# Fused local-global attention and gated long convolution on one core: the filter's spectrum and the inverse tables move into the attention of batch 0

## The chip, the cores and the metric

The kernel runs on one core of a Trainium2 chip. The metric is the device time of one execution in microseconds. A profile is one execution recorded by the hardware profiler; its span is the time from the first to the last recorded instruction.

## What is computed

Inputs q, k, v are (4, 8, 768, 64): 4 batches, 8 heads, 768 positions, 64 features. Attention is causal and local over 96 positions, plus the first 8 positions for everybody, with a slope per head times the distance as bias:

```python
is_global = pos[None, :] < 8
is_local = (rel >= 0) & (rel < 96)
keep = is_global | is_local
dist = where(is_global & ~is_local, 96, abs(rel))
scores = q @ k.T / 8 - slope[h] * dist
a = softmax(where(keep, scores, -1e9))
x = (a @ v), heads side by side: (4, 768, 512)
```

Its output goes through a gated long convolution ("Hyena"), with one filter for all batches:

```python
x1, x2, x3 = split(x @ w_proj)                 # 512 to 3 * 512
conv = irfft(rfft(x2) * rfft(filter_fft))      # along the 768 positions
out = (x1 * conv * x3) @ w_out                 # float32
```

## The kernel before

**Tiles and stages.** Keys and values of a batch are held in seven tiles of 128 rows: rows 0 to 7 of each tile are the 8 global positions, rows 8 to 127 are 120 positions of their own. For each pair of heads, attention transposes queries and keys on PE (`transpose_q`, `transpose_k`), makes scores in three groups (`weights`, L497), takes the exponential on ACT (L504), multiplies by a mask on DVE (`masked`, L513 and L516, put off by one step), multiplies by the values (`values`, L524 and L529), divides by the sum (L533, L534), and transposes the result into `xT` (`transpose_x`, L541 and L542). After two pairs, `butterfly` (L444, L445) adds and subtracts the two halves of the sequence into `xa` and `xb`; the last butterfly of a batch is what `hyena` reads first (L573).

`hyena` projects `xa` and `xb` with the middle third of `w_proj` (L573, L575), transforms them by matrices (`forward`, L328, six slots: four of 128 frequency rows, two of 64 and 64), multiplies by the filter's spectrum h1, h2 (`product`, `sums`, L588 to L598), transforms back with the inverse tables (L637), multiplies by the gates (`gate`, L559 to L564, with the outer thirds of `w_proj`), and multiplies by `w_out` (L655 to L659).

**The filter stage.** `filter_stage` is ten steps: one that adds and subtracts the filter's halves (L342, L343), six `forward` steps whose result is written into h1 and h2 with scales and signs (L349 to L365), and three that transpose the forward tables into the inverse ones (`inverse_tables`, L287 to L294).

**The order of the work.** Each engine runs its instructions in the order in which the program emits them. `weave` mixes several generators: each gets a start, an end and a number of steps, and the one with the smallest share so far emits the next step. `after(n, fn)` puts a piece of work off: with n = 1 it is emitted at the end of the next woven step. Attention 0 runs alone (L709). Then for each batch b, `hyena` of b and attention of b + 1 are woven (L712 to L723); for b = 0 the filter stage is a third stream with a start at 0.12 and an end at 0.4, and `hyena` emits four gates early. In attention 0 a dummy matmul (`busy`, L280) follows each step.

**PSUM.** `mm` gives out three buffers; in attention 0 the transposes use these too (`tr`), later ones have a buffer of their own.

**Queues.** Nearly all loads go through GpSimd's queue (POOL in the profile), because they convert float32 to float16: values 0, two pairs of heads, the three thirds of `w_proj` (`load_weights`), then `load_batch(1)`: keys 1, queries 1, the filter, values 1; then `w_out`, then batch 2. The 8 global rows of tiles 1 to 6 are copied from tile 0: for batches 1 to 3 by a DMA on SP's queue (L111), for batch 0 by a DVE copy inside attention (L424). The loads of tiles 1 to 6 take 128 rows, of which the first 8 are then overwritten. Keys and queries of batch 0 come in another layout and are not touched by the change.

Of the kernel before, what the change touches and what calls it, by code (L numbers as in the profile page):

```python
# [17 lines left out]
P = 128  # L18
# [26 lines left out]
class Fused:  # L45
# [53 lines left out]
    def load_tiles(self, dst, src, b):  # L99

        g, D = self.nc.gpsimd, self.D
        for t in range(7):
            lo = max(0, self.K0[t] - NG)
            hi = self.K0[t] + KL
            g.dma_start(dst[P - (hi - lo):P, t, :, 0:D],  # L105
                        src[b, :, lo:hi, :].rearrange("h p d -> p h d"))
            if t == 0:
                g.dma_start(dst[0:NG, 0, :, 0:D],
                            src[b, :, 0:NG, :].rearrange("h p d -> p h d"))
        if b > 0:  # L110
            self.nc.sync.dma_start(dst[0:NG, 1:7], dst[0:NG, 0:1].to_broadcast(  # L111
                [NG, 6] + list(dst.shape[2:])))

    def load_batch(self, b):
        g = self.nc.gpsimd
        qt, kt, vt = self.batch_tiles()
        self.load_tiles(kt, self.k, b)
        for t in range(6):
            g.dma_start(qt[:, t], self.q[b, :, P * t:P * t + P, :].rearrange("h p d -> p h d"))  # L119
        if b == 1:  # L120
            self.load_filter()
        self.load_tiles(vt, self.v, b)
        return qt, kt, vt
# [37 lines left out]
    def load_weights(self):  # L161
        g, cp, DM = self.nc.gpsimd, self.cp, self.DM
        self.w = cp.tile([P, 4, 3 * DM], F16)
        self.wr = self.w_proj.rearrange("(t p) n -> p t n", p=P)
        for o in (DM, 0, 2 * DM):
            g.dma_start(self.w[:, :, o:o + DM], self.wr[:, :, o:o + DM])
# [115 lines left out]
    def inverse_tables(self):  # L282
# [3 lines left out]
        for sp in range(3):  # L286
            tp = self.ps.tile([P, 1024], F16, tag="tr", bufs=1)  # L287
# [48 lines left out]
    def filter_spectrum(self):  # L336
# [10 lines left out]
        sc = 2.0 * H_SCALE  # L347

        def evac(s, pt):  # L349
            if s < 4 and s % 2 == 0:  # L350
                nc.scalar.mul(self.h1[:, s], pt, sc)
                nc.vector.tensor_scalar(self.h1[:, s + 1], pt, sc, None, op0=Alu.mult)
                if s == 0:
                    nc.scalar.mul(self.h1[0:1, 0], pt[0:1], H_SCALE)
            elif s < 4:
                nc.scalar.mul(self.h2[:, s - 1], pt, sc)
                nc.vector.tensor_scalar(self.h2[:, s], pt, -sc, None, op0=Alu.mult)
                if s == 1:
                    nc.scalar.mul(self.h1[0:1, 1], pt[0:1], H_SCALE)
# [402 lines left out]
```

## Time and profile before

| | |
|---|---|
| timed runs, us | 221.43, 223.82, 224.78 (median 223.82) |
| profiled execution, us | 222.22 |
| its span, us | 220.4 |
| PE busy | 193.8 us (88%) |
| DVE busy | 148.5 us (67%) |
| ACT busy | 153.3 us (70%) |
| POOL busy | 75.8 us (34%) |
| granted TensorE clock, mean | 0.997 |
| loaded and stored by DMA | 20.90 MB |

A row of the view by groups reads: line, engine, operation, output <- input, shapes and count, then busy us and mean ns of one, then the engine's idle time before them and what ended it. A row of the timeline begins with the start and the length in us; what stands in brackets is the idle time before it and the releaser. Buffer names carry numbers: h_814 is h1, h_815 is h2, f_793 and f_794 are the filter's sum and difference.

### The profile page before, as it was taken

The page shows a single profiled execution, that of the slowest core. Times are in us where ns is not written, and L with a number is a line of the kernel's source. Part 1 is how long each engine was busy: PE and PEld are TensorE (multiplying, and loading weights), DVE is VectorE, ACT ScalarE, POOL GpSimd, SP SyncE. Part 2 cuts the span into 40 slices and gives each one's busy share as a digit, 9 for nine tenths or more (in the row PEclk, how much of TensorE's full clock was granted, in tenths as well). Part 3 has the DMA queues.
Part 4 walks back from the last instruction along what each step waited for, and adds up shares of the span by engine and source line. Part 5 has one row for each costly group of instructions (what it writes and reads, how often), then busy time and mean ns, then how long its engine had stood idle before and what let it go on. Part 6 is the DMA issues. An engine that isn't in the chain of part 4 may idle for free.

```text
span 220.4 us, 4260 instructions
## 1 busy us (share of the span) xinstructions
PE 193.8 (88%) x1661; PEld 104.5 (47%) x1661; DVE 148.5 (67%) x321; ACT 153.3 (70%) x249; POOL 75.8 (34%) x102
## 2 busy tenths in 40 slices
PE   7588986897798968689899999998999999998982
PEld 2243554443455535334455656444555555454630
DVE  6966677564695999822299999334998991078630
ACT  6996685487656767547978685767877847673742
POOL 7999379758795000599540000000000000000000
PEclk9999999999999999999999999999999999999998
DMA  6999999999999800299999000520000006100025
GB/s 195 145 140 184 207 155 155 192 128 166 155 137 122 32 9 3 17 150 231 212 130 39 8 3 1 190 98 0 3 0 3 0 1 241 48 0 0 3 84 204
DMA packets 79573, 20.90 MB, mean 95 GB/s; under 512 B 71328, under 2 KB 76480, under 8 KB 79552
## 3 DMA queue, kind: packets, MB, share of 16 engines
q0 software_dynamic: 74672, 12.46, 91.3%
q1 hardware_dynamic: 4880, 8.16, 11.0%
q8 instruction: 13, 0.21, 0.4%
q14 instruction: 8, 0.07, 0.1%
HBM read 26.48 MB, written 6.29 MB: 149 GB/s over the span
## 4 chain that ended last, share of the span: by engine, by line
PE 31%; DVE 30%; DMA 18%; POOL 8%; ACT 7%; issue 4%; POOLq 0%; DVEq 0%; SPq 0%
PE pt L655 7%; PE pt L559 7%; DMA w<-in_moe_w_proj_dram 5%; DMA vt<-in_v_dram 5%; PE pt L573 5%; DVE g L564 5%; DVE xn L534 4%; DMA fl<-in_moe_filter_fft_dram 4%; DMA vt<-vt 3%; PE pt L637 3%; POOL qt L119 2%; ACT E_104 L504 2%; PE sp L497 2%; DVE E_107 L516 2%; PE pt L328 2%
## 5 line engine op out<-in xcount | busy, mean ns | idle before, releaser
L559 PE MATMUL pt<-xT,w 128*128 128x384 f16 x256 | 46.8, 326 | 0.6 <-DVE g L564 0.4
L559 PEld LDWEIGHTS <-w 128*128 128x128 f16 x256 | 23.4, 98 | 16.7 <-issue 2.5
L105 POOL DMA_DIRECT2D vt<-in_v_dram x28 | 25.2, 913 | 7.6 <-DMA qt<-in_q_dram 4.0
L504 ACT ACTIVATE E_107<-sp 128x864 f16<-128x864 f32 x24 | 21.5, 894 | 7.1 <-PE sp L497 6.6
L655 PE MATMUL pt<-wo,y 128*128 128x512 f16 x96 | 22.2, 379 | 2.6 <-DVE y L648 1.7
L497 PE MATMUL sp<-QT,KT 64*128 64x216 f16 (+2 forms) x224 | 18.2, 254 | 5.9 <-ACT E_104 L504 2.8
L658 ACT ACTIVATE t<-pt 128x512 f32<-128x512 f32 x24 | 14.3, 597 | 13.0 <-PE pt L655 12.9
L504 ACT ACTIVATE E_104<-sp 128x864 f16<-128x864 f32 x24 | 21.5, 897 | 2.4 <-PE sp L497 1.8
L105 POOL DMA_DIRECT2D kt<-in_k_dram x21 | 19.6, 953 | 5.8 <-DMA w<-in_moe_w_proj_dram 4.8
L534 DVE TENSOR_TENSOR xn<-o,rc 128x448 f16<-128x448 f32 x32 | 20.0, 624 | 1.1
L637 PE MATMUL pt<-inv,X 128*128 128x384 f16 x96 | 18.5, 326 | 1.1 <-DVE X L598 1.1
L575 ACT CAST dst<-pt 128x512 f16<-128x512 f32 x24 | 14.2, 593 | 6.8 <-PE pt L573 6.8
L497 PEld LDWEIGHTS <-KT 64*128 64x128 f16 x224 | 7.7, 95 | 23.6 <-issue 19.5
L328 PE MATMUL pt<-dst,fwd 128*128 128x512 f16 x72 | 18.9, 380 | 0.0
L542 ACT COPY xT<-tr 128x768 f16<-128x768 f16 x16 | 12.8, 798 | 7.7 <-PE tr L541 7.6
L601 ACT CAST X<-pt 128x512 f16<-128x512 f32 x24 | 14.1, 588 | 5.5 <-PE pt L328 5.1
L280 PE MATMUL pt<-idle 128*128 128x512 f16 x35 | 16.4, 475 | 1.4 <-DVE warm L682 1.2
L516 DVE TENSOR_TENSOR E_104<-E_104,mask 128x864 f16<-128x864 f16 x16 | 9.7, 604 | 10.4 <-ACT E_104 L504 9.9
L119 POOL DMA_DIRECT2D qt<-in_q_dram x18 | 15.8, 916 | 1.2 <-DMA kt<-in_k_dram 1.1
L655 PEld LDWEIGHTS <-y 128*128 128x128 f16 x96 | 8.9, 98 | 13.3 <-DVE y L648 2.9
L486 DVE COPY KT<-tr 128x896 f16<-128x896 f16 x12 | 7.4, 619 | 10.9 <-PE tr L485 10.9
L541 PE MATMUL tr<-ident,xn 128*128 128x128 f16 x112 | 9.0, 220 | 5.2 <-DVE xn L534 4.8
(231 smaller groups left out, 381.9 us busy)
## 6 DMA issues: line engine op xcount, KB each, us to landing
out_dram<-t SPq DMA_DIRECT2D x24, 256.0 KB, 2.4
vt<-in_v_dram POOLq DMA_DIRECT2D x24, 128.0 KB, 7.4
kt<-in_k_dram POOLq DMA_DIRECT2D x18, 128.0 KB, 7.5
qt<-in_q_dram POOLq DMA_DIRECT2D x18, 128.0 KB, 7.2
w<-in_moe_w_proj_dram POOLq DMA_DIRECT2D x3, 512.0 KB, 10.3
t<-in_q_dram SPq DMA_DIRECT2D x2, 384.0 KB, 4.2
t<-in_k_dram SPq DMA_DIRECT2D x2, 384.0 KB, 5.2
fl<-in_moe_filter_fft_dram POOLq DMA_DIRECT2D x1, 768.0 KB, 9.3
```

The source lines that it names most:

```text
L105: g.dma_start(dst[P - (hi - lo):P, t, :, 0:D], src[b, :, lo:hi, :].rearrange("h p d -> p h d"))
L119: g.dma_start(qt[:, t], self.q[b, :, P * t:P * t + P, :].rearrange("h p d -> p h d"))
L280: self.nc.tensor.matmul(pt, self.idle[:, 0:P], self.idle, start=True, stop=True)
L328: self.nc.tensor.matmul(pt, self.fwd[:, kt, s, :], src[:, kt, :], start=(kt == 0), stop=(kt == 2))
L497: nc.tensor.matmul(sp[:, hh, off:off + w], KT[64 * hh:64 * hh + 64, o:o + P], QT[64 * hh:64 * hh + 64, KL * m:KL * m + w], start=(off == 0 ...
L504: nc.scalar.activation(eo, sp[:, :, 0:432].rearrange("p h (m w) -> p h m w", m=2), Act.Exp, scale=self.scale)
L534: nc.vector.tensor_mul(xn[:, :, hh, :], o[:, :, 0:D], rc.to_broadcast([P, 7, D]))
L559: nc.tensor.matmul(pt[:, 0:h], self.w[:, c, o + P * j:o + P * j + P], xT[:, c, h * s:h * s + h], start=(c == 0), stop=(c == 3))
L575: nc.scalar.copy(dst[:, t, :], pt)
L637: nc.tensor.matmul(pt[:, 0:h], X[:, s, cs], self.inv[:, s, :], start=(s == slots[0]), stop=(s == slots[-1]))
L655: nc.tensor.matmul(pt, y[:, c, P * t:P * t + P], self.wo[:, c, :], start=(c == 0), stop=(c == 3))
L658: nc.scalar.mul(ot, pt, osc)
```

## The change

- The filter stage is woven into attention 0, from the share 0.7 to 1 of it, instead of into Hyena 0; Hyena 0 no longer emits four gates early. The inverse tables' transposes use the three `mm` buffers.
- The filter's load is issued behind the first third of `w_proj`, ahead of keys 1. The two outer thirds (the gates' weights) and `w_out` are issued behind values 1.
- The 8 global rows are loaded first, tiles 0 to 6 take 120 rows each, and the copy to tiles 1 to 6 is a DMA on SP's queue for all batches, batch 0 among them; the DVE copy L424 is gone.
- In the filter stage, each PSUM result is read once by one engine (ACT for h1 of slots 0, 2, 4, 5, DVE for h2); the second copy, or the one with the other sign, is made by DVE from the float16 result in SBUF, partly put off by one step (`second`). The special first row gets its scale from two small per-row tables.

```diff
--- before.py
+++ after.py
@@ -99,17 +99,13 @@
     def load_tiles(self, dst, src, b):
 
         g, D = self.nc.gpsimd, self.D
+        g.dma_start(dst[0:NG, 0, :, 0:D], src[b, :, 0:NG, :].rearrange("h p d -> p h d"))
+        self.nc.sync.dma_start(dst[0:NG, 1:7], dst[0:NG, 0:1].to_broadcast(
+            [NG, 6] + list(dst.shape[2:])))
         for t in range(7):
-            lo = max(0, self.K0[t] - NG)
-            hi = self.K0[t] + KL
-            g.dma_start(dst[P - (hi - lo):P, t, :, 0:D],
-                        src[b, :, lo:hi, :].rearrange("h p d -> p h d"))
-            if t == 0:
-                g.dma_start(dst[0:NG, 0, :, 0:D],
-                            src[b, :, 0:NG, :].rearrange("h p d -> p h d"))
-        if b > 0:
-            self.nc.sync.dma_start(dst[0:NG, 1:7], dst[0:NG, 0:1].to_broadcast(
-                [NG, 6] + list(dst.shape[2:])))
+            lo = self.K0[t]
+            g.dma_start(dst[NG:P, t, :, 0:D],
+                        src[b, :, lo:lo + KL, :].rearrange("h p d -> p h d"))
 
     def load_batch(self, b):
         g = self.nc.gpsimd
@@ -117,9 +113,11 @@
         self.load_tiles(kt, self.k, b)
         for t in range(6):
             g.dma_start(qt[:, t], self.q[b, :, P * t:P * t + P, :].rearrange("h p d -> p h d"))
+        self.load_tiles(vt, self.v, b)
         if b == 1:
-            self.load_filter()
-        self.load_tiles(vt, self.v, b)
+            for part in (0, 2):
+                self.load_w_in(part)
+            self.load_w_out()
         return qt, kt, vt
 
     def load_first(self):
@@ -159,11 +157,12 @@
         return t
 
     def load_weights(self):
-        g, cp, DM = self.nc.gpsimd, self.cp, self.DM
-        self.w = cp.tile([P, 4, 3 * DM], F16)
-        self.wr = self.w_proj.rearrange("(t p) n -> p t n", p=P)
-        for o in (DM, 0, 2 * DM):
-            g.dma_start(self.w[:, :, o:o + DM], self.wr[:, :, o:o + DM])
+        self.w = self.cp.tile([P, 4, 3 * self.DM], F16)
+        self.load_w_in(1)
+
+    def load_w_in(self, part):
+        o, wr = part * self.DM, self.w_proj.rearrange("(t p) n -> p t n", p=P)
+        self.nc.gpsimd.dma_start(self.w[:, :, o:o + self.DM], wr[:, :, o:o + self.DM])
 
     def load_filter(self):
         g, DM = self.nc.gpsimd, self.DM
@@ -284,7 +283,7 @@
         nc = self.nc
         self.inv = self.cp.tile([P, 6, 384], F16)
         for sp in range(3):
-            tp = self.ps.tile([P, 1024], F16, tag="tr", bufs=1)
+            tp = self.tr(True)
             for c in range(2):
                 for a in range(3):
                     nc.tensor.transpose(tp[:, 384 * c + P * a:384 * c + P * a + P],
@@ -345,24 +344,34 @@
         self.h1 = cp.tile([P, 6, DM], F16)
         self.h2 = cp.tile([P, 6, DM], F16)
         sc = 2.0 * H_SCALE
+        s0, s1 = (self.sp.tile([P, 1], F32, bufs=1, name=f"s{i}") for i in range(2))
+        for t, x in ((s0, H_SCALE), (s1, 0.0)):
+            nc.vector.memset(t, sc)
+            nc.vector.memset(t[0:1], x)
+
+        c, a, h = self.h1, self.h2, slice(0, 64)
+
+        def second(s):
+
+            if s < 4:
+                nc.vector.tensor_scalar(a[:, s], a[:, s - 1], -1.0, None, op0=Alu.mult)
+            else:
+                nc.vector.tensor_copy(c[64:P, s], c[h, s])
+                nc.vector.tensor_scalar(a[64:P, s], a[h, s], -1.0, None, op0=Alu.mult)
 
         def evac(s, pt):
             if s < 4 and s % 2 == 0:
-                nc.scalar.mul(self.h1[:, s], pt, sc)
-                nc.vector.tensor_scalar(self.h1[:, s + 1], pt, sc, None, op0=Alu.mult)
-                if s == 0:
-                    nc.scalar.mul(self.h1[0:1, 0], pt[0:1], H_SCALE)
+                nc.scalar.mul(c[:, s], pt, sc if s else s0)
             elif s < 4:
-                nc.scalar.mul(self.h2[:, s - 1], pt, sc)
-                nc.vector.tensor_scalar(self.h2[:, s], pt, -sc, None, op0=Alu.mult)
+                nc.vector.tensor_scalar(a[:, s - 1], pt, sc if s > 1 else s1, None, op0=Alu.mult)
+                nc.vector.tensor_copy(c[:, s], c[:, s - 1])
                 if s == 1:
-                    nc.scalar.mul(self.h1[0:1, 1], pt[0:1], H_SCALE)
-                    nc.vector.memset(self.h2[0:1, 0:2, :], 0.0)
+                    nc.vector.tensor_scalar(c[0:1, 1], pt[0:1], H_SCALE, None, op0=Alu.mult)
             else:
-                nc.scalar.mul(self.h1[0:64, s], pt[0:64], sc)
-                nc.scalar.mul(self.h1[64:P, s], pt[0:64], sc)
-                nc.vector.tensor_scalar(self.h2[0:64, s], pt[64:P], sc, None, op0=Alu.mult)
-                nc.vector.tensor_scalar(self.h2[64:P, s], pt[64:P], -sc, None, op0=Alu.mult)
+                nc.scalar.mul(c[h, s], pt[h], sc)
+                nc.vector.tensor_scalar(a[h, s], pt[64:P], sc, None, op0=Alu.mult)
+            if s % 2 or s == 4:
+                self.after(1, lambda: second(s))
         for s in range(6):
             self.forward(s, f2[0], f2[1], evac)
             yield 1
@@ -420,9 +429,6 @@
         cast(1)
         yield 1
         for i in range(n + 1):
-            if first and i == 1:
-                self.nc.vector.tensor_copy(vt[0:NG, 1:7], vt[0:NG, 0:1].to_broadcast(
-                    [NG, 6, self.H, self.D + 1]))
             for live, fn in ((i < n, lambda: sc(i, 0)),
                              (i + 1 < n, lambda: trk(i + 1)),
                              (i < n, lambda: sc(i, 1)),
@@ -705,15 +711,14 @@
         self.load_tiles(qkv[2], self.v, 0)
         self.load_pairs(2, nc.gpsimd, F16)
         self.load_weights()
+        self.load_filter()
         x = self.new_x()
-        self.weave((self.attention(*qkv, *x, first=(cast, ths)), 34, 0, 1))
+        self.weave((self.attention(*qkv, *x, first=(cast, ths)), 34, 0, 1),
+                   (self.filter_stage(), 10, 0.7, 1))
         loads = [qkv, self.load_batch(1)]
-        self.load_w_out()
         for b in range(self.B):
-            streams = [(self.hyena(b, *x, early=4 if b == 0 else 0), 30, 0, 1)]
+            streams = [(self.hyena(b, *x, early=0), 30, 0, 1)]
             nx = None
-            if b == 0:
-                streams.insert(0, (self.filter_stage(), 10, 0.12, 0.4))
             if b + 2 < self.B:
                 loads.append(self.load_batch(b + 2))
             if b + 1 < self.B:
```

## The prediction

> **What bounds the kernel now.** I read the busy time stage by stage first, because the page's 88% for PE is a mean over unlike stages. Columns: PE, PEld, DVE, ACT, POOL busy us (instructions), granted clock, DMA share, GB/s.
>
> ```profile
> 31.65:41.50 9.85, 7.42 (x105) 4.57 (x106) 6.39 (x15) 5.48 (x8) 9.62 (x12) 1.00 2.18 168
> 41.50:99.80 58.30, 48.29 (x433) 26.10 (x431) 41.67 (x83) 38.34 (x65) 30.95 (x39) 1.00 1.75 97
> 99.80:142.90 43.10, 41.93 (x399) 23.43 (x397) 31.30 (x67) 32.62 (x55) 10.03 (x12) 1.00 1.14 99
> 142.90:186.00 43.10, 41.92 (x393) 23.26 (x391) 31.29 (x67) 32.50 (x55) 0.00 (x0) 1.00 0.10 37
> ```
>
> The second row is Hyena of batch 0 beside attention 1 and the filter; the third and fourth are the same pair of streams for the next batches, without the filter. They take 43.1 us and PE is busy for 41.9 of them: PE-bound. The batch-0 stage takes 58.3 with PE idle for 10. Its surplus over the third row is 6.4 us on PE, 10.4 on DVE, 5.7 on ACT.
>
> The PE timeline gives the exact ends, and shows two places where other things than PE decide.
>
> ```profile
> 41.49 0.59 PE L573 MATMUL pt<-w,xa 128*128 128x512 f16 x2
> 42.37 0.60 PE L573 MATMUL pt<-w,xa 128*128 128x512 f16 x2 [0.29 <-DVE xa L444]
> ...
> 59.90 0.20 PE L524 MATMUL o<-vt,E_104 128*128 128x65 f16 x1 [0.86 <-DMA vt<-vt]
> ...
> 61.67 0.81 PE L328 MATMUL pt<-f_794,fwd 128*128 128x512 f16 x3
> ...
> 64.57 0.49 PE L290 MATMUL tp<-ident,fwd 128*128 128x128 f16 x6
> ...
> 99.83 1.03 PE L573 MATMUL pt<-w,xa 128*128 128x512 f16 x4
> 108.70 1.47 PE L559 MATMUL pt<-xT,w 128*128 128x384 f16 x8
> 142.88 1.03 PE L573 MATMUL pt<-w,xa 128*128 128x512 f16 x4
> ```
>
> So Hyena 0 really starts at 42.37, when the last butterfly is there; Hyena 1 starts at 99.83, Hyena 2 at 142.88. From the chain of waits comes the other limit, a line of transfers:
>
> ```profile
> 17.03 12.04 DMA w<-in_moe_w_proj_dram
> ...
> 35.54 9.31 DMA fl<-in_moe_filter_fft_dram
> ...
> 45.14 7.32 DMA vt<-in_v_dram
> ...
> 52.60 7.25 DMA vt<-vt
> ```
>
> Three weight parts landed by 29.07, the filter by 44.85, the last of values 1 by 52.46, and only then the row copy `vt<-vt` could go, because the old tiles 1 to 6 also write rows 0 to 7. PE waited 0.86 us for it. Filter work could not start before 44.85 in any place.
>
> **Part 1, the filter leaves the batch-0 stage.** What remains there is instruction for instruction the stream of batch 1 (early=0, the same two streams, the same shares). I cost it by that stage: 142.88 − 99.83 = 43.05 us. Two of the 24 matmuls of L573 run ahead of the held one, as at 41.49 now; four take 1.03 and a single one 0.38 (L328's mean below), so starts are 0.22 apart and I take 0.4 off: 42.65 from the held matmul. Now it is 99.83 − 42.37 = 57.46. **Gain 14.8 us.** The four early gates that go back are inside that comparison. Bounds: 13.8 if 1 us of the start is not copied, 15.2 if none of the 0.4 is double counted.
>
> **Part 2, the filter enters the end of attention 0.** The weave gives attention a step of 1/34 and the filter a start at 0.7, so the first filter step follows attention's 24th, the third score group of head pair 2; then the two alternate, ten filter steps against eleven. On the old clock that is 31.65 to 41.75. The rows for what is moved (busy us in total, mean ns):
>
> ```profile
> L328 PE MATMUL pt<-f_793,fwd 128*128 128x512 f16 x9 | 2.4, 380 | 0.0
> L352 DVE TENSOR_SCALAR h_814<-pt 128x512 f16<-128x512 f32 x2 | 1.4, 688 | 0.7 <-ACT h_814 L351 0.7
> L364 DVE TENSOR_SCALAR h_815<-pt 64x512 f16<-64x512 f32 x2 | 1.4, 692 | 1.6 <-ACT h_814 L363 1.6
> L351 ACT ACTIVATE h_814<-pt 128x512 f16<-128x512 f32 x2 | 1.2, 606 | 0.0
> L342 DVE TENSOR_TENSOR f_793<-fl 128x1536 f16<-128x1536 f16 x1 | 0.9, 946 | 0.0
> L292 DVE COPY inv<-tp 128x768 f16<-128x768 f16 x3 | 1.7, 551 | 1.1 <-PE tp L290 1.1
> ```
>
> And DVE's timeline for the small copies and for the window itself:
>
> ```profile
> 1.22 0.08 DVE L227 MEMSET cst<- 1x1 f16 x3
> ...
> 17.85 0.57 DVE L146 COPY t<-t 128x768 f16<-128x768 f16 x1 [1.51 <-DMA t<-in_q_dram]
> 18.81 0.36 DVE L146 COPY t<-t 128x768 f16<-128x768 f16 x1 [0.40 <-DMA t<-in_k_dram]
> ...
> 19.61 0.95 DVE L424 COPY vt<-vt 8x3120 f16<-8x3120 f16 x1
> ...
> 21.50 0.44 DVE L481 COPY KT<-KT 128x56 f16<-128x56 f16 x1
> ...
> 26.58 0.62 DVE L146 COPY t<-t 128x768 f16<-128x768 f16 x2
> ...
> 28.82 0.17 DVE L481 COPY KT<-KT 128x56 f16<-128x56 f16 x1
> ...
> 31.01 0.63 DVE L534 TENSOR_TENSOR xn<-o,rc 128x448 f16<-128x448 f32 x1
> ...
> 39.64 0.62 DVE L534 TENSOR_TENSOR xn<-o,rc 128x448 f16<-128x448 f32 x1
> 41.75 0.56 DVE L444 TENSOR_TENSOR xa<-xT 128x768 f16<-128x768 f16 x1 [1.49 <-ACT xT L542]
> ```
>
> DVE decides here; its added work is:
> - sum and difference of the filter, two of L342's kind at 0.946, 1.90;
> - PSUM reads for slots 1, 3, 4, 5 and the one-row fix: 5 × 0.69 = 3.45. The one-row form (1x512) isn't in the trace on DVE; I price it by its length like its neighbours, between 0.2 (the 56-element copy) and 0.69;
> - eight short f16 copies and products inside SBUF (512 elements): not in the trace. Above a 56-element copy (0.17), below a 768-element one (0.31 to 0.57). I take 0.27 each, 2.2 in all, near the undisturbed 0.31; bounds 0.2 and 0.5, so 1.6 to 4.0;
> - three inverse copies, 3 × 0.551 = 1.65; four tiny memsets at 0.08, 0.3.
>
> That is 9.5 us, with bounds 8.4 and 11.3. DVE is busy 6.39 of 9.85 us there, idle 3.46; of the last wait (1.49, from 40.26) 1.24 lies in the window and is latency, transpose then ACT copy, that stays, though the last inverse copy now fits beneath it. So 2.2 to 2.8 us of idle time takes in new work. **Cost 7.2 us** (9.5 − 2.3). I walked the emitted order too: sum and difference hold the third mask product back to 33.5, the forward matmuls' PSUM buffer (three, rotating with attention's transposes) was always read in time, and the last butterfly began at about 48.7, 6.95 later. Bounds: 6.0, and 11.3 if nothing fits into idle time. PE's added 5 us (18 matmuls at 0.22, 18 short transposes) and ACT's 2.4 (four copies at 0.6) lie under DVE's: in the window PE has 7.42 of 9.85 busy, ACT 5.48, and the window grows by 7.
>
> A copy's own time depends on its neighbour: the 56-element one took 0.44 at 21.50 and 0.17 at 28.82, the 768-element ones 0.57, 0.36 and 0.31. GpSimd was issuing loads during all of them.
>
> The Trainium skill, page SBUF — State Buffer, section Who interferes with whom, says that VectorE in its two-port modes and GpSimd take a shared port pair in turns and the loser blocks wholly. It speaks against this change, which puts eight such copies under the issue of keys, queries and values 1. By that rule at its worst each copy would cost the disturbed 0.5, 1.8 us more than my sum, 216.4 in place of 214.6. The trace agrees that the same copy takes 0.17 to 0.44, not that GpSimd is the reason.
>
> **Part 3, the loads.** The filter takes the place of weight parts 0 and 2:
>
> ```profile
> 15.59 1.44 POOL w L166 x2
> ```
>
> The view of tile w up to 100 us has the landing times:
>
> ```profile
> DMA to landing us min/median/max: 8.0/10.3/12.0
> ```
>
> The first part lands about 8.0 us after its issue, near 24.3, the third at 29.07. The filter is 768 KB where the other two were 1024 KB, so it lands before 29.07; its first reader comes at 31.65. Cover 2.6 us, cost nothing. Keys 1, queries 1 and values 1 keep their order and come no later; parts 0 and 2 land where the last of values 1 did, by 52.5. The first gate (L559) comes 108.70 − 99.83 = 8.9 us into the stage, so at 49.6 + 8.5 = 58.1. Cover 5.6 us, cost nothing; w_out follows and is read 35 us later. If the cover went, each late microsecond would stop PE. POOL's clearing of the ones column for batch 2 waits on the same queue for attention 0's last values, now 7 us later; its loads are read only from 92 on.
>
> **Part 4, rows by DMA.** For batches 1 to 3 the copy need not wait for the other tiles, so the 0.86 us wait at 59.90 goes; that is already in the gain. For batch 0 a DVE copy (L424, 0.95) becomes a transfer:
>
> ```profile
> 6.26 1.24 POOL L108 DMA_DIRECT2D vt<-in_v_dram  x1
> ```
>
> ```profile
> 21.29 0.32 PE L524 MATMUL o<-vt,E_104 128*128 128x65 f16 x2
> ```
>
> ```profile
> DMA to landing us min/median/max: 3.5/6.2/10.7
> ```
>
> The 8-row load now goes first, issued by about 6.4, lands 3.5 to 10.7 later (tile vt up to 62 us; median 6.2), and the copy takes what `vt<-vt` took from its issue, 7.25: it is there between 17.2 and 24.4, at the median by 19.9. It is read from 21.29. So 0, or a stall of up to 3.1; L424's own time was off the path, since PE came to the values at its own pace. I take 0, bounds −0.95 and +3.1. Queued behind it on SP are only the copies of keys 1 and values 1, needed 20 us later.
>
> The Trainium skill, page DMA: Bandwidth & Descriptors, section on why a DMA increments its semaphore by 16, lets a 120-row tile use fewer than the 16 engines a 128-row tile uses, with as many rows on each. By that rule the rows no longer loaded save no time; by bytes they'd save some 5% of 7 us per tensor, under covers anyway. Both give the same sum; no run here shows it.
>
> **Sum.** The profiled execution: 222.22 − 14.8 + 7.2 = 214.6. The three timed runs have a median of 223.82, 1.6 above it, and a lowest of 221.43; I put half that offset on, **215.4**.
>
> **Rivals.** (a) *The tail serialises.* DVE, ACT and PE are in order; if each filter step waits for its matmuls, its reader and the correction after it before attention goes on, a step costs 0.81 + 0.69 + 0.3, six times, plus 1.9 and three times 0.49 + 0.55: 16 us, and none of it fits the gaps. Time 222.22 − 14.8 + 16 = 223.4, with the offset 224.2; slower from a tail of 14.8 on. For: L364 waited 1.6 for ACT in the old code. Against: three PSUM buffers, and the corrections are put off by a step. (b) *Batch 0 is held by transfers anyway*: if parts 0 and 2 land only near 65 the gates stop PE for 7 us, 214.6 + 7 + 0.8 = 222.4. For: the page's DMA row, 5.5 us a digit, stays nearly full until 77 us.
>
> ```profile
> DMA  6999999999999800299999000520000006100025
> ```
>
> Against: nothing is put ahead of them that was not there before. (c) *The row copy for batch 0 is late* by the full 3.1: 218.5. (d) *The change moves more into the gaps than I allow*, tail 5, 213.2.
>
> **Chances.** Forecast 0.72; (a) 0.08, of which half is slower than before; (b) 0.08; (c) 0.07; (d) 0.05. Low: tail 6.0 and gain 15.2 give 213.0; the lowest run's offset, −0.8, and the 0.95 of L424 make it 211.3, and I write 211.5. High: tail 11.3 with the offset, 222.22 − 14.8 + 11.3 + 0.8, is 219.5. It leaves out (a) and (b). Over 2% is about what a measurement here can tell from no change; faster means below 219.3. Faster 0.85, within 2% 0.11, slower 0.04.
>
> **What would show it.** The held L573 of Hyena 0 near 49.6 (DVE near 9 tenths from 32 on), Hyena 1's first L573 near 92.2 with a stage of 42.7 that has PE busy about 41.9, the later stages at 43.1 as now; no wait on `fl`, on `w` at the first gate, or on `vt<-vt`. Wrong: a stage of batch 0 above 45; a tail above 11; a DMA wait at the first value product of attention 0.

## The result, and the profile after

The changed kernel takes 212.38 us (median of 211.79 to 213.18), the kernel before 224.14 in the same runs: a ratio of 0.9517, with a 95% interval of 0.9451 to 0.9584. Its profiled execution took 211.79 us with a span of 210.0; the one before, 222.22 with 220.4. The forecast was 215.4, range 211.5 to 219.5. One execution, the first profile of "rows of values 0 by DVE" below, ran 275.13 us at a granted clock of 0.765 and is left out.

Line numbers are those of each kernel's own file: L573 has become L579, L559 L565, L444 L450, L534 L540. The stages of the changed kernel, columns as before (PE, PEld, DVE, ACT, POOL busy, clock, DMA share, GB/s):

```profile
29.60:46.20 16.60, 12.57 (x141) 7.24 (x142) 15.28 (x38) 7.75 (x12) 16.58 (x22) 1.00 2.52 140
46.90:89.50 42.60, 41.55 (x394) 23.34 (x395) 31.76 (x69) 32.02 (x54) 22.89 (x27) 1.00 1.52 112
89.50:132.50 43.00, 41.83 (x395) 23.34 (x394) 31.29 (x67) 32.55 (x55) 13.24 (x16) 1.00 1.23 104
```

The stage of batch 0 now reads like that of batch 1, PE busy 41.55 of 42.6. The end of attention 0 has become a stretch in which DVE is busy 15.28 of 16.6 us. PE's timeline has the exact ends:

```profile
46.97 0.60 PE L579 MATMUL pt<-w,xa 128*128 128x512 f16 x2 [0.29 <-DVE xa L450]
...
55.08 1.47 PE L565 MATMUL pt<-xT,w 128*128 128x384 f16 x8
...
89.25 1.03 PE L579 MATMUL pt<-w,xa 128*128 128x512 f16 x4
...
132.29 1.03 PE L579 MATMUL pt<-w,xa 128*128 128x512 f16 x4
```

Hyena 0 begins at 46.97 (before 42.37) and hands over at 89.25 (before 99.83). DVE's timeline shows how the tail went:

```profile
29.09 0.62 DVE L540 TENSOR_TENSOR xn<-o,rc 128x448 f16<-128x448 f32 x1
29.63 0.95 DVE L341 TENSOR_TENSOR f_513<-fl 128x1536 f16<-128x1536 f16 x1
...
33.77 0.43 DVE L367 COPY h_529<-h_529 128x512 f16<-128x512 f16 x1
34.23 0.68 DVE L369 TENSOR_SCALAR h_529<-pt 1x512 f16<-1x512 f32 x1
...
39.54 0.72 DVE L359 COPY h_529<-h_529 64x512 f16<-64x512 f16 x1
40.19 0.27 DVE L360 TENSOR_SCALAR h_530<-h_530 64x512 f16<-64x512 f16 x1
...
41.11 0.60 DVE L522 TENSOR_TENSOR E_107<-E_107,mask 128x864 f16<-128x864 f16 x1
...
46.35 0.56 DVE L450 TENSOR_TENSOR xa<-xT 128x768 f16<-128x768 f16 x1 [1.02 <-ACT xT L548]
```

The fourth division of attention 0 (xn) begins at 29.09; in the old profile it is the same instruction at 31.01. It is the last mark ahead of all filter work, and I use it below as the tail's start. From it to the last butterfly's xa the old kernel took 41.75 − 31.01 = 10.74, the new one 46.35 − 29.09 = 17.26.

The 0.62 us from that xa to the held matmul is the same in both.

So the 10.4 us between the two spans are made of: 1.92 before the mark, −6.52 in the tail (lost), 57.46 − 42.28 = 15.18 in the stage of batch 0, and −0.18 from there to the end (120.57 before, 120.75 now).

### The profile page after: what moved, and what is told of

It reads as the page before. It is cut to its first block, busy times and chain, and to the rows that moved or that the text cites. A ratio compares the mean times of both kernels' runs of the same rounds, so it can differ in the third digit from the quotient of the medians.

```text
span 210.0 us, 4253 instructions
## 1 busy us (share of the span) xinstructions
PE 189.5 (90%) x1661; PEld 102.7 (49%) x1661; DVE 147.0 (70%) x328; ACT 149.7 (71%) x243; POOL 75.6 (36%) x102
## 4 chain that ended last, share of the span: by engine, by line
DVE 48%; PE 29%; ACT 8%; issue 5%; DMA 5%; POOL 3%; POOLq 0%; DVEq 0%
DVE xn L540 9%; PE pt L661 7%; PE pt L579 7%; DVE g L570 6%; PE pt L565 4%; DVE E_107 L522 3%; DMA t<-in_k_dram 3%; DMA vt<-in_v_dram 2%; DVE E_107 L519 2%; PE tr L547 2%; DVE rc L539 2%; ACT E_104 L510 2%; DVE y L651 2%; PE tr L491 2%; PE pt L643 2%
## 5 line engine op out<-in xcount | busy, mean ns | idle before, releaser
L565 PE MATMUL pt<-xT,w 128*128 128x384 f16 x256 | 46.5, 327 | 0.0
L565 PEld LDWEIGHTS <-w 128*128 128x128 f16 x256 | 23.3, 98 | 15.9 <-issue 1.6
L107 POOL DMA_DIRECT2D vt<-in_v_dram x28 | 25.7, 944 | 1.4 <-DMA qt<-in_q_dram 0.8
L664 ACT ACTIVATE t<-pt 128x512 f32<-128x512 f32 x24 | 14.3, 598 | 12.0 <-PE pt L661 11.8
L107 POOL DMA_DIRECT2D kt<-in_k_dram x21 | 19.0, 915 | 10.3 <-DMA fl<-in_moe_filter_fft_dram 4.2
L540 DVE TENSOR_TENSOR xn<-o,rc 128x448 f16<-128x448 f32 x32 | 20.0, 624 | 1.1
L279 PE MATMUL pt<-idle 128*128 128x512 f16 x35 | 15.1, 436 | 1.3 <-DVE warm L688 1.2
L579 PE MATMUL pt<-w,xa 128*128 128x512 f16 x48 | 12.2, 380 | 0.3 <-DVE xa L450 0.3
## 6 DMA issues: line engine op xcount, KB each, us to landing
fl<-in_moe_filter_fft_dram POOLq DMA_DIRECT2D x1, 768.0 KB, 11.9
```

The lines of the kernel that those rows point to most:

```text
L107: g.dma_start(dst[NG:P, t, :, 0:D], src[b, :, lo:lo + KL, :].rearrange("h p d -> p h d"))
L279: self.nc.tensor.matmul(pt, self.idle[:, 0:P], self.idle, start=True, stop=True)
L540: nc.vector.tensor_mul(xn[:, :, hh, :], o[:, :, 0:D], rc.to_broadcast([P, 7, D]))
L565: nc.tensor.matmul(pt[:, 0:h], self.w[:, c, o + P * j:o + P * j + P], xT[:, c, h * s:h * s + h], start=(c == 0), stop=(c == 3))
L579: nc.tensor.matmul(pt, src[:, c, P * t:P * t + P], self.w[:, c, DM:2 * DM], start=(c == 0), stop=(c == 3))
```

## The experiments

Each kernel is the changed one with one edit, except where it says otherwise. Times are medians; the tail is from the fourth xn to the last xa, the stage from Hyena 0's held matmul to Hyena 1's first. "Filler short" is the moment from which the 512-column filler matmuls of attention 0 take 0.4 us in place of 0.6, for good up to 30 us. The kernel before was measured again in every set, with medians from 223.1 to 224.1; the ratio is to the one of the same set.

| kernel | us | ratio to before (95%) | filler short | 4th xn | tail | stage of batch 0 |
|---|---|---|---|---|---|---|
| before | 223.1 to 224.1 | 1 | 25.0 | 31.01 | 10.74 | 57.46 |
| changed, first profile | 212.38 | 0.9517 (0.9451 to 0.9584) | 18.1 | 29.09 | 17.26 | 42.28 |
| changed, second | 213.54 | 0.9561 (0.9516 to 0.9606) | 25.6 | 31.57 | 18.30 | 42.29 |
| rows of values 0 by DVE, first | 213.54 | 0.9559 (0.9511 to 0.9606) | | | | |
| rows of values 0 by DVE, second | 213.0 | 0.9554 (0.9515 to 0.9592) | 21.8 | 29.69 | 17.45 | 42.30 |
| filter stage in batch 0 | 221.0 | 0.9875 (0.980 to 0.995) | 25.6 | 31.58 | 10.75 | 56.44 |
| inverse tables on ACT | 212.69 | 0.9508 (0.9452 to 0.9563) | 22.9 | 30.07 | 17.90 | 42.29 |
| old order of loads | 227.84 | 1.0198 (1.0115 to 1.028) | 24.7 | 30.68 | | 42.29 |
| four PSUM reads to ACT | 211.9 | 0.9489 (0.9455 to 0.9523) | 24.6 | 30.62 | 16.43 | 42.29 |
| old kernel, more filler | 223.9 | 1.0026 (0.9992 to 1.0061) | 18.1 | 31.31 | 10.66 | 58.07 |
| GpSimd quiet in the tail | 221.95 | 0.9961 (0.9919 to 1.0002) | 23.7 | 30.29 | 16.61 | 51.64 |
| h1's copies on ACT too | 213.95 | 0.9591 (0.9537 to 0.9645) | 18.1 | 29.12 | 18.11 | 42.29 |
| the same, filter from 0.62 | 217.87 | 0.9749 (0.970 to 0.9799) | 23.2 | | | 42.29 |
| old way to write the spectrum | 216.12 | 0.9707 (0.9645 to 0.977) | 21.7 | 29.54 | 20.15 | 42.28 |

### Where the filter's work stands: e2_filter_in_batch0

```diff
-        self.weave((self.attention(...), 34, 0, 1),
-                   (self.filter_stage(), 10, 0.7, 1))
+        self.weave((self.attention(...), 34, 0, 1))
...
+            if b == 0:
+                streams.insert(0, (self.filter_stage(), 10, 0.12, 0.4))
```

Also early=4 and the old PSUM buffer for the transposes.

> The changed kernel with the filter stage woven into batch 0 again (0.12 to 0.4, four early gates); loads, row transfers and the new way to write the spectrum stay as changed. First theory: what shrank the stage of batch 0 by 15 us is that the filter's work left it. Then this loses that gain and gets the tail back: 212.4 + 15.1 - 6.6 = 220.9 (219.5 to 223), stage of batch 0 at 55 to 57.5. Rival: the earlier values 1 and row copies shrank it, the filter's place does little: 212 to 216, stage of batch 0 below 49.

221.0 us. PE's timeline:

```profile
42.95 0.60 PE L579 MATMUL pt<-w,xa 128*128 128x512 f16 x2 [0.29 <-DVE xa L450]
...
99.39 1.03 PE L579 MATMUL pt<-w,xa 128*128 128x512 f16 x4
```

The stage is 56.44 again, 1.0 below the old one: that is what earlier values, row copies and the new way to write the spectrum are worth there (the old PE wait of 0.86 for `vt<-vt` is gone). The other 14.2 us are the filter's place together with the four early gates, which go back with it. The first theory holds.

### What its load's place is worth: e4_old_load_order

```diff
-        self.load_w_in(1)
+        for part in (1, 0, 2):
+            self.load_w_in(part)
...
+        if b == 1:
+            self.load_filter()      # behind queries 1, ahead of values 1
         self.load_tiles(vt, self.v, b)
```

`load_batch(1)`, which has the filter's load in it here, is emitted ahead of the weave.

> The changed kernel with the old order of loads: all three weight parts ahead of keys 1, the filter behind queries 1, w_out behind values 1. First theory: the new place of the filter stage needs the new place of its load; the sum of the filter then waits on DVE until the filter lands, near 44 to 45 instead of 29.6, and everything behind it in DVE's order waits too: 212.4 + 14 = 226.5 (223 to 229), slower than before. Rival: attention goes on around the wait, since only filter steps need the filter: within 2 us of 212.4.

227.84 us, slower than before by 1.2 to 2.8%, from two executions. DVE's timeline:

```profile
44.72 0.96 DVE L342 TENSOR_TENSOR f<-fl 128x1536 f16<-128x1536 f16 x1 [13.42 <-DMA fl<-in_moe_filter_fft_dram]
```

DVE stands for 13.42 us with attention's masks and divisions queued behind the filter's sum, though they need no filter. Moving the load is thus a condition of moving the work. The stage of batch 0 is as short as in the changed kernel, 42.29: what is lost lies all ahead of it.

### The copy of the rows: e1_rows_on_dve and e1b_rows_on_dve

```diff
-        self.nc.sync.dma_start(dst[0:NG, 1:7], dst[0:NG, 0:1]...)
+        if b > 0:
+            self.nc.sync.dma_start(dst[0:NG, 1:7], dst[0:NG, 0:1]...)
...
+            if first and i == 1:
+                self.nc.vector.tensor_copy(vt[0:NG, 1:7], vt[0:NG, 0:1]...)
```

> The changed kernel, but the eight global rows of values 0 are spread by the DVE copy inside attention 0 again (0.95 us) instead of by the transfer. First theory: the 2.0 us by which attention 0 ran ahead of the old profile before any filter work (sum of the filter at 29.63, where the old profile ended the same value product at 31.64) come from PE, whose 512-column filler matmul fell from 0.63 to 0.39 us at 17.8 instead of at 24.2, and that moment shifts from one execution to the next; the copy was off the path. Then the time stays within 0.5 us of the changed kernel's 212.4, and Hyena 0's held matmul is at 47.0 where the filler gets short near 18, later by some 2 us where it gets short near 24. Rival: the copy's removal gave the 2.0 us. Then 213.4 to 214.4, with the held matmul at 48 to 49 however early the filler gets short.

213.54 us. The first theory had put the copy off the path altogether; 1.2 us more than the 212.38 of the earlier runs spoke for the rival, so both were measured again side by side, with the theory altered.

> The changed kernel with the DVE copy of the eight rows of values 0 back (0.95 us), once more, since its first profile had PE at 0.77 of its clock throughout. First theory, as the first runs have altered it: the copy lies on DVE's path when PE is fast at 20 us (in the changed kernel DVE has no gap from 19.1 to 23.6), and beside it when PE is slow. Then 0.5 to 1.0 more than the changed kernel in the same call, and the fourth xn 0.9 later if the filler is short from 18 on. Rival: off the path in all cases, 0 within 0.3.

213.0 us, beside 213.54 for the changed kernel on the same chip: no difference that these runs can tell (the two ratios' intervals almost coincide, and each is 0.8 to 0.9% wide, 2 us). The 0.5 to 1.0 more that the altered theory gave isn't there in the medians. Its profile doesn't test the rest of it: the filler gets short only at 21.8, so PE was still slow at 20 us, and the fourth xn at 29.69 is where the kernel with the old way to write the spectrum, without the copy and short from 21.7, has it (29.54). A profile with the copy and a fast PE comes below, in the old kernel with more filler.

### The moment at which PE gets fast: after_again and e6_more_filler

> The changed kernel once more, unaltered, beside the others on one chip. First theory: how early attention 0 gets through its first pairs goes by the moment at which the filler matmul falls from 0.63 to 0.39 us, which differs between executions of one kernel. Then the time is 211.8 to 213.4, and the start of the fourth division (xn, 29.09 in the first profile) is at 29.0 to 29.3 if the filler is short from 18 on, at 30 to 31.6 if it gets short only at 22 to 25. Rival: the moment is set by the program, and it repeats: short from 18.1, xn at 29.1.

213.54 us for the same code, and the profile fell on the slowest of its six executions, 215.37, which is used here because it shows where the 3.6 us to the first profile lie: 2.5 ahead of the mark and 1.0 in the tail. The filler matmuls of attention 0 in the first profile, and in the second:

```profile
16.20 1.25 PE L279 MATMUL pt<-idle 128*128 128x512 f16 x2
...
18.10 0.39 PE L279 MATMUL pt<-idle 128*128 128x512 f16 x1
```

```profile
18.27 0.61 PE L279 MATMUL pt<-idle 128*128 128x512 f16 x1
...
24.58 0.62 PE L279 MATMUL pt<-idle 128*128 128x512 f16 x1
25.58 0.39 PE L279 MATMUL pt<-idle 128*128 128x512 f16 x1
```

And the two marks on DVE in the second:

```profile
31.57 0.62 DVE L540 TENSOR_TENSOR xn<-o,rc 128x448 f16<-128x448 f32 x1
...
40.58 0.83 DVE L367 COPY h<-h 128x512 f16<-128x512 f16 x1
...
49.87 0.56 DVE L450 TENSOR_TENSOR xa<-xT 128x768 f16<-128x768 f16 x1 [1.02 <-ACT xT L548]
```

Same instructions, but PE takes 0.6 us for a 512-column matmul until 25 us instead of 18, and the mark comes at 31.57 instead of 29.09. In the old kernel's profile the long ones last until 24 us:

```profile
23.07 0.63 PE L280 MATMUL pt<-idle 128*128 128x512 f16 x1
...
25.02 0.39 PE L280 MATMUL pt<-idle 128*128 128x512 f16 x1
```

The changed kernel itself has profiles on both sides of the old one, and the table shows what orders them: in the ten profiles of the changed kernel and its variants that have both, the mark rises with the moment at which the filler gets short for good, from 29.09 at 18.1 to 31.58 at 25.6. The old kernel's 31.01 at 25.0 lies between its neighbours in this order (30.68 at 24.7, 31.57 at 25.6). So the 1.92 us ahead of the mark go with the moment, which the first theory said, and the profiled pair shows no other effect of the change there. What sets the moment stays open: one profile of the old kernel can't tell whether the change shifts it on average. An attempt to bring the moment forward by hand, in the kernel before:

```diff
                     if first:
-                        self.busy(1)
+                        self.busy(2 if i == 0 else 1)
```

> The kernel before with two filler matmuls in place of one after each step of the first head pair, so that PE is busier from 11 to 18 us. First theory: PE gets fast when it has been busy enough, and 2 us of the difference between the two profiles is that. Then the filler is short from 18 us on or earlier, the fourth xn starts at 29.0 to 30.2 instead of 31.0, and the time is 221 to 222.5, 1 to 2 less than before. Rival: the filler's own time (six times 0.43) is paid: 224 to 226.

223.9 us, no gain. The filler is short from 18.09 on, but the mark stays at 31.31:

```profile
20.46 0.60 DVE L516 TENSOR_TENSOR E<-E,mask 128x864 f16<-128x864 f16 x1
20.98 1.14 DVE L424 COPY vt<-vt 8x3120 f16<-8x3120 f16 x1
22.05 0.88 DVE L479 COPY KT<-tr 128x720 f16<-128x720 f16 x1
...
31.31 0.62 DVE L534 TENSOR_TENSOR xn<-o,rc 128x448 f16<-128x448 f32 x1
```

That is 2.22 later than in the first profile of the changed kernel, where the filler is short from 18.1 too. The rows show where the 2.2 us are. The queries of the next pair arrived later, DVE having waited 2.90 us for them until 19.24 (18.01 there), so this mask product starts at 20.46 and not at 19.12: 1.34. And from it to the copy of the keys it takes 1.59 us and not 0.69, because the DVE copy of the rows (L424) stands between them: 0.90. So with a fast PE this copy is on the path, as the altered theory of the section before had it. Why the load came later, and whether more filler makes PE fast earlier, is not settled by one profile, since the first profile of the changed kernel has it at 18 without.

### What decides the tail: e3, e5, e8, e9 and e10

Three copies off DVE:

```diff
-            nc.vector.tensor_copy(self.inv[...], tp[:, 0:768])
+            nc.scalar.copy(self.inv[...], tp[:, 0:768])
```

> The changed kernel with the three inverse-table copies on ACT instead of DVE. First theory: DVE decides the end of attention 0 (15.28 us busy of 16.6). Then three copies of 0.55 leave its path, the last butterfly comes 1.1 to 1.7 earlier and the time is 210.7 to 211.3. Rival: the chain from mask to value product to transpose decides, DVE only fills; or ACT, in order, pays it back. Then 212.4 within 0.4.

212.69 us, no gain, as the rival said. In its profile PE got slow again for a while, so that the stretch is longer than it had to be:

```profile
43.77 0.85 PE L289 MATMUL tr<-ident,fwd 128*128 128x128 f16 x6
```

(0.50 in the changed kernel's.) But the medians don't fall either. These copies stand behind the last mask product; that the chain mask, values, division, transpose sets the pace there and they only fill it is the rival's reading, and with the slow stretch this profile doesn't show it by itself.

Work ahead of that mask product, off DVE:

```diff
-                    nc.vector.tensor_scalar(c[0:1, 1], pt[0:1], H_SCALE, ...)
+                    nc.scalar.mul(c[0:1, 1], pt[0:1], H_SCALE)
...
-                nc.vector.tensor_scalar(a[:, s - 1], pt, sc, ...)      # s = 3
+                nc.scalar.mul(a[:, s - 1], pt, sc)
...
-                nc.vector.tensor_scalar(a[h, s], pt[64:P], sc, ...)    # s = 4, 5
+                nc.scalar.mul(a[h, s], pt[64:P], sc)
```

> The changed kernel with four of the five reads of PSUM in the filter stage moved from DVE to ACT (the one-row fix, h2 of slots 3, 4 and 5): 2.7 us less on DVE and 2.4 more on ACT, ahead of the last mask product, which waited for DVE. First theory: DVE's work up to that mask product decides the tail (PE waited 1.49 us for it). Then the tail from the fourth xn to the last butterfly falls from 17.3 by 1.0 to 2.2, and the time by as much. Rival: ACT, in order, holds back the last exponential by what DVE saves: within 0.5 of the changed kernel.

211.9 us, all six executions between 211.15 and 212.66; the changed kernel beside it 213.54, and 212.38 in its first runs. The tail is 16.43:

```profile
30.62 0.63 DVE L543 TENSOR_TENSOR xn<-o,rc 128x448 f16<-128x448 f32 x1
...
41.28 0.61 DVE L525 TENSOR_TENSOR E<-E,mask 128x864 f16<-128x864 f16 x1
41.92 0.84 DVE L359 COPY h<-h 64x512 f16<-64x512 f16 x1
...
47.05 0.56 DVE L453 TENSOR_TENSOR xa<-xT 128x768 f16<-128x768 f16 x1 [1.02 <-ACT xT L551]
```

From the mark to the last mask product it is 10.66 now, 12.02 in the changed kernel. The tail is 0.8 shorter than in one profile of the changed kernel and 1.9 shorter than in the other, of 2.7 us taken away. The eight short copies and products account for the two values. They take 3.83 us in this profile, 1.58 more than the undisturbed 2.25 of e7_pool_quiet below. By these sums the tail undisturbed would be 14.85, against 16.61 there: an estimate of 1.8 for the 2.7. DVE decides, but not alone. This is the fastest version measured here (its interval against the changed kernel's of the same runs just overlaps, so that it is faster is not shown).

More of the same kind, h1's second copies read from PSUM by ACT:

```diff
-                nc.vector.tensor_copy(c[64:P, s], c[h, s])
...
                 nc.scalar.mul(c[:, s], pt, sc if s else s0)
+                nc.scalar.mul(c[:, s + 1], pt, sc)
...
-                nc.vector.tensor_copy(c[:, s], c[:, s - 1])
...
+                nc.scalar.mul(c[64:P, s], pt[h], sc)
```

With the one-row fix and slot 3's read on ACT too, slots 4 and 5's h2 on DVE.

> The changed kernel with more of the filter stage on ACT: the second copies of h1 (slots 1, 3 and the lower halves of 4 and 5) are read from PSUM by ACT instead of copied by DVE inside SBUF, and h2 of slot 2 and the one-row fix too. DVE has 3.1 us less or, with its copies disturbed, 4; ACT 3.6 more. First theory: DVE's work decides the tail, and it falls from 17.3 to 18.3 to 14.5 to 15.5; time 210.3 to 211.5, 1.0 to 2.5 less than the changed kernel. Rival: ACT, now as full as DVE, holds back the exponentials: 212 to 213.5.

213.95 us, tail 18.11: no gain over the changed kernel (213.54; tails 17.26 and 18.30), which is the rival's side, though 0.5 above its range. DVE, now with less to do, waits for ACT, whose queue puts the exponentials behind the copies:

```profile
34.22 0.61 DVE L525 TENSOR_TENSOR E<-E,mask 128x864 f16<-128x864 f16 x1 [0.33 <-ACT E L513]
...
35.56 0.68 DVE L522 TENSOR_TENSOR E<-E,mask 128x432 f16<-128x432 f16 x2 [0.53 <-ACT E L513]
...
41.33 0.69 DVE L375 TENSOR_SCALAR h<-pt 64x512 f16<-64x512 f32 x1 [0.62 <-ACT h L374]
```

Then the start of the stage, in that kernel:

```diff
-                   (self.filter_stage(), 10, 0.7, 1))
+                   (self.filter_stage(), 10, 0.62, 1))
```

> The one before, with the filter stage from 0.62 of attention 0 instead of 0.7, three attention steps earlier. First theory: there is DVE idle time between 24 and 29 us to be filled, and the filter lands at 28.0, so at most 1 us is gained, and only where PE got fast late: 0.3 to 1.0 less than the one before. Rival: the sum of the filter now waits for the filter and holds DVE's queue: 0.5 to 2 more.

217.87 us, 3.9 worse, and for a reason that neither theory had. The filter is there in time; the sum starts at 30.14 with no wait. But ACT's first copy of the spectrum now stands ahead of an exponential and waits 2.76 us for DVE, and PE behind it. What it waits for is one of the small per-row tables (`s`, a memset of 0.06 us) that DVE has queued behind the filter's sum and a division; in the changed kernel the same wait is 1.02. No run has this memset ahead of the sum.

```profile
32.97 0.69 ACT L363 ACTIVATE h<-pt,s 128x512 f16<-128x512 f32 x1 [2.76 <-DVE s L349]
```

```profile
38.47 0.36 PE L506 MATMUL sp<-QT,KT 64*128 64x216 f16 x4 [2.81 <-ACT E L513]
```

At last the old way to write the spectrum in the new place (the old `evac`, L349 to L365 of before):

> The changed kernel with the old way to write the spectrum (each PSUM result read by ACT and by DVE, four on each engine more or less, and row fixes that wait for the other engine). DVE's work is the same as in the new way within 0.5 us (6.1 against 6.2 to 7.7 us), ACT has 3.6 more. First theory: DVE decides, so the new way is worth little: 212 to 214, within 1 us of the changed kernel. Rival: the waits between ACT and DVE in the old way (0.7 to 1.6 us each, seen in the old profile) come on the path now: 214 to 217.

216.12 us, the rival's range, and a tail of 20.15, 2.9 more than in the changed kernel's first profile and 1.9 more than in its second. DVE's work is hardly more (16.10 us busy in the tail, 15.79 in the changed kernel's first), but ACT and DVE take turns at one result:

```profile
35.20 0.69 DVE L370 TENSOR_SCALAR h<-pt 128x512 f16<-128x512 f32 x1 [0.97 <-ACT h L369]
...
37.79 0.69 DVE L365 TENSOR_SCALAR h<-pt 128x512 f16<-128x512 f32 x1 [0.80 <-ACT h L364]
...
44.09 0.61 DVE L526 TENSOR_TENSOR E<-E,mask 128x864 f16<-128x864 f16 x1
```

Such turns hold up attention's work behind them: from the mark to the last mask product it is 14.55 us here and 12.02 in the changed kernel's first profile, so 2.5 of the 2.9 lie there. (Behind it PE was slow again for a while, with a granted clock of 0.50 from 46 to 48, which is part of the rest.) By the medians it is 2.6 us, 216.12 against 213.54, and the intervals of the two ratios lie apart. So the new way to write the spectrum carries some 2 to 3 us of the change. It differs in two things, one reader for each PSUM result and corrections put off by a step, and this run takes both back; the waits shown speak for the first.

### The short copies: e7_pool_quiet

```diff
+        if b == 1:
+            g.memset(self.z, 0.0)          # after DVE's last inverse copy, by DVE's memset of z
         self.load_tiles(vt, self.v, b)
```

> The changed kernel, but GpSimd waits for the last inverse copy before it issues values 1 and what follows, so that it issues nothing from about 35 to 45 us. It is to show why the same short copy inside SBUF took 0.28 in one place and 0.43 to 0.83 in another. First theory: DVE's copies and GpSimd's issue of loads hold each other up. Then all eight short copies and products after 36 us take 0.25 to 0.31, and the tail from the fourth xn to the last butterfly is 16.5 to 17.0 (17.26 and 18.30 in the two profiles of the changed kernel). Rival: they wait for something else (ACT's writes, the semaphores); then some still take 0.5 to 0.8. Values 1 come 10 us later, so PE may wait for them at the first value product of batch 1, up to 4 us, and the time is no measure: 212 to 217.

GpSimd issues nothing from 34.6 to 45.95, and every short copy on DVE is short:

```profile
34.97 0.28 DVE L372 COPY h<-h 128x512 f16<-128x512 f16 x1
...
36.41 0.27 DVE L362 TENSOR_SCALAR h<-h 128x512 f16<-128x512 f16 x1
...
38.56 0.28 DVE L372 COPY h<-h 128x512 f16<-128x512 f16 x1
...
40.57 0.29 DVE L364 COPY h<-h 64x512 f16<-64x512 f16 x1
```

The eight add up to 2.25 us; in the changed kernel's profiles to 2.90 and 3.95. Its tail is 16.61, and 16.61 + 0.65 = 17.26, 16.61 + 1.70 = 18.31: the two tails of the changed kernel to 0.01. A third profile agrees: with the rows of values 0 by DVE the eight take 3.09, and 16.61 + 0.84 = 17.45 is its tail. It is GpSimd's issue and not the traffic: from 34.6 to 37.0 GpSimd issued nothing while transfers still ran at 147 GB/s, and both copies in that stretch are short; in the kernel with the old order of loads GpSimd stood idle from 46.7 to 58.9, and all eight took 0.28 to 0.29, the first two with 158 GB/s around them. The first theory holds as far as DVE goes; that GpSimd is held up in turn is not shown. The time, 221.95, is not a gain: the outer thirds of `w_proj` come 11 us later, and the first gate has to wait for them.

```profile
61.35 1.46 PE L570 MATMUL pt<-xT,w 128*128 128x384 f16 x4 [5.66 <-DMA w<-in_moe_w_proj_dram]
63.89 1.46 PE L570 MATMUL pt<-xT,w 128*128 128x384 f16 x4 [1.08 <-DMA w<-in_moe_w_proj_dram]
```

The stage of batch 0 grows to 51.64. I had expected a wait for values 1; it was for the weights queued behind them.

## Why the prediction was right, and where it was off

**The gain in batch 0: right.** 14.8 forecast, 15.18 measured. Costing the stage by its twin of batch 1 was good to 0.4 us, and 42.28 to 42.30 came back in every kernel whose loads were in time, whatever had happened before.

**The tail: right in size.** 7.2 forecast, a growth of the tail; 17.26 − 10.74 = 6.5 in one profile, 18.30 − 10.74 = 7.6 in the other. The terms: the one-row read, bounded by 0.2 and 0.69, took 0.68; the eight short operations, taken as 2.2 with bounds 1.6 and 4.0, took 2.90 and 3.95, the second near the upper bound, because of GpSimd's issue. PE's and ACT's work did lie under DVE's, as the step said, but ACT only just: with some 3.6 us more on it (the copies of h1) DVE waited for ACT and the saving on DVE gained nothing.

**The rule on the port pair: borne out on DVE's side.** The prediction gave the eight copies 1.8 us more by the Trainium skill's page SBUF — State Buffer, section Who interferes with whom. Measured were 0.65 and 1.70 above the quiet 2.25. With GpSimd quiet all eight took 0.27 to 0.29; with GpSimd issuing, 0.27 to 0.83. The trace agrees that DVE's copies are held up beside GpSimd's issue; it does not show by which port, nor GpSimd being held up.

The prediction misread its own trace here. It said that GpSimd was issuing loads during all the copies that it compared. In that profile GpSimd stood idle from 24.7 to 27.3 and from 28.2 to 29.4, and the quick copies, at 26.58 and 28.82, fell into these gaps; the slow ones at 17.85 and 21.50 fell into issues. The old trace already pointed at GpSimd.

**The loads: right, with less cover.** The filter was issued at 16.11 and landed 11.9 later, at 28.0; its reader came at 29.63, so 1.6 us of cover, not 2.6 (all of attention 0 came 1.9 earlier in this profile). The view of tile fl up to 40 us:

```profile
DMA to landing us min/median/max: 11.9/11.9/11.9
```

With the old order the same step costs 13.4 us of DVE's time. The gates did not wait: the outer thirds were issued by 43.5 and took at most 9.5 us to land, so they were there by 53.0, and the first gate came at 55.08. That is a cover of 2.1 us or more, where 5.6 was forecast. Had the weights been late by more than their cover, rival (b) would have been true, as the quiet GpSimd showed by accident.

**The rows by DMA: right for this profile.** The copy went out at 9.88, and the first product of values 0 at 20.44 waited for nothing:

```profile
9.88 0.88 SPq L103 DMA_DIRECT2D vt<-vt  x1
```

```profile
20.44 0.23 PE L530 MATMUL o<-vt,E_104 128*128 128x65 f16 x2
```

That the DVE copy was off the path, as the prediction said, holds where PE is slow at 20 us, as in the profile before; in the old kernel with more filler, where PE was fast, it took 0.9 us of the path.

**Rival (a) was nearer than I thought.** I gave the serialised tail 16 us and 0.08. The new `evac` keeps it off; with the old one the tail grew by 20.15 − 10.74 = 9.4. The prediction priced the rewriting of `evac` only by its DVE time. Against this rival it named the corrections put off by a step, but not that the turns between ACT and DVE go.

**The sum: 3.0 us too high, inside the range.** For the profiled pair it gave 214.6 and 211.79 was measured, 2.8 less: 1.92 ahead of the mark, 0.7 in the tail, 0.4 in the stage of batch 0, less 0.2 behind it. The term that was mis-sized is the one that wasn't there: attention 0 up to the mark, taken as unchanged, came out 1.92 earlier. A second profile of the same kernel has it 0.56 later, so that is mostly the draw of one execution and no effect to be forecast. The half offset, 0.8, was about right: the median of the changed kernel is 0.6 above its profiled execution, which leaves 0.2 of the 3.0. What the medians give beside the pair's 10.4 us (11.8 in the first runs, 9.6 where the changed kernel was run again) differs from it by less than that draw. Of the 2.5 us that loads, rows and the spectrum's writing gave without the filter's move (221.0 against 223.5), the profiles account for 1.0; the rest is left open.

## What to carry to other kernels

Work that can stand in a stretch where its engine is idle is worth moving out of one where another engine is the bound, and a later stage with the same instructions is the best price list for what is left. Move its load first, and count what an in-order engine has queued behind each wait: here the same move was worth about 10 to 12 us, or cost 4, by the order of the loads. In the new place the form of the work mattered as well as its sum: here one reader for each PSUM result was the better form, with no more copies on ACT than leave the exponentials room.

## What the runs showed of the hardware

The time of a 512-column matmul falls from 0.63 to 0.39 us somewhere between 18 and 25.6 us, at a different place in two profiles of the same code. In four profiles it fell at 18.1, rose again to 0.61 to 0.63 for some 3 us, and then fell for good (with the inverse tables on ACT: 0.39 at 18.09, 0.63 at 19.90, 0.38 at 22.86; also with the old order of loads, with four PSUM reads on ACT, and with the filter from 0.62). The mark in attention 0 goes with the last fall, over 2.5 us. The column of the granted clock doesn't show the first slow stretch: it is 1.00 from 17.7 to 25.0 in the profile of before, where the matmuls were slow, and in the first of after, where they were fast. It does show the return: with the inverse tables on ACT it is 0.50 from 19.5 to 22.5, and 0.77 over 17.7 to 25.0. So a column at 1.00 early in a profile has to be checked against the length of a matmul. The Trainium skill, page TensorE: Matmul & The Clock Gate, part 1, says that the array runs at half rate until it has been busy for a window of 3.4 us, and that the window runs free of the kernel's start. The trace agrees with two rates and with a moment that shifts from run to run; how busy such a window must be these profiles don't settle. In both profiles of the changed kernel PE was busy for 2.7 of the 4 us from 10 to 14 and for all of 14 to 16; in one it was fast at 18.1, in the other only at 25.6, after being busy without a gap from 20 to 25.

A short copy inside SBUF on DVE takes 0.28 us alone and up to 0.83 while GpSimd issues loads; eight of them made 1 us between two executions of one kernel.
